# Token-major scores, exponentials turned by DMA, and hand-made orders in an attention and gated feed-forward kernel

## The chip, the cores and the metric

The kernel runs on one core of a Trainium2 chip. The metric is the device time of one execution in microseconds (us); the time of a kernel is the median of its runs. The core's engines work side by side, each through its own list of instructions in order: TensorE (PE in the profile, its weight loads PEld), VectorE (DVE), ScalarE (ACT), GpSimd (POOL) and SyncE (SP), which issues DMA transfers; "SPq" is SP's instruction queue. An instruction waits for the work that it needs, and everything behind it on its engine waits too. PSUM, into which TensorE writes, has eight banks of 128 x 512 numbers.

## The reference

```python
def _attn_ref(q, kv, w_sr):                # q 4 x 12288 x 128, kv 4 x 384 x 32 x 128
    r = 4
    kv_pool = kv.reshape(B, H // r, r, W // r, r, C).mean(axis=(2, 4))
    kv_flat = kv_pool.reshape(B, -1, C) @ w_sr        # 768 keys an image
    k = v = kv_flat
    s = scale * (q @ k.transpose(0, 2, 1))
    a = np.exp(s - s.max(-1, keepdims=True))
    a /= a.sum(-1, keepdims=True) + 1e-09
    return a @ v
def _moe_ref(x, w_gate, w_val, w_out):     # 128 -> 1536 -> 128
    gate = np.maximum(x @ w_gate, 0.0)
    val = x @ w_val
    return gate * val @ w_out
```

Four images of 12,288 query tokens each attend to 768 pooled keys, which are the values too; each token's result goes through a feed-forward layer whose hidden vector is a rectified gate times a value. The layer is of degree two in x: if x is scaled by c, the output is scaled by c squared.

## The kernel before, in words

The 49,152 tokens are cut into 96 tiles of 512, four tiles to a group. All matmul operands are 16 bit. For each tile there are five steps.

- Scores (`scores`, line 290): keys are the weights, the turned queries stream through; the result has keys on the partitions and tokens along the row. Six chunks of 128 keys, one matmul of 512 columns and one exponential on ACT (line 295) each, which writes `aT`.
- Values (`values`, line 297): each 128 x 128 block of `aT` is loaded as weights, and the 128 value columns and a column of ones stream through it, 129 columns. 24 such matmuls a tile; the last column gives the row sums. `keep_sums` and `keep_values` (lines 311 to 324) invert the sums and scale the result on DVE, and `x_turn` (line 326) has SP turn it by a DMA transpose into `xT`.
- Gate and value projections (lines 372 to 390): 12 matmuls of 512 columns each. ACT casts each value block to 16 bit, and DVE forms max(gate, 0) times value into `hT`.
- Output projection (`out_proj`, line 398): 12 matmuls of 512 columns, added up in one bank.
- `out_turn` (line 411): DVE turns the output in 32 x 32 blocks, POOL scales it, and SP stores it in four DMAs.

The first four tiles (`LEAD`) are handled differently: `lead_values` streams `aT` through the values as weights, which gives the result already turned and not divided by the sums; `lead_sums` and `lead_scales` form the squared inverse sums, and `out_turn` multiplies the outputs by them (line 421).

The queries come by POOL's DMAs, cast on the way (`q_load`), and are turned by SP's DMA transposes, one of 128 x 2048 per group (`q_turn`, line 119). The keys of the first image are pooled, turned by TensorE, projected and turned again in an opening whose order is a list of words (`OPENING`, line 69). Those of the other three are made beside the main loop, in pairs of 128-key chunks: four loads of 512 KB (`kv_load`), sums on POOL (`pool_pixels`), 32 x 32 turns on DVE with a detour through DRAM (`turn_blocks`: a write "placed", four reads), a projection by TensorE (`project`), and two lone 128 x 128 DMA transposes for the values (`turn_values_dma`, line 282).

The main loop (line 610) runs once per tile k in twelve steps. In each step the output projection of tile k-4, the value projection of k-3, a score of k or two value chunks of k-1, and the gate projection of k-3 stand in turn, so that TensorE always finds work whose inputs are ready. PSUM banks are handed out in rotation from one pool of eight:

```python
    psum = ctx.enter_context(tc.tile_pool(name="psum", bufs=8, space=bass.MemoryType.PSUM))
    def bank(shape, dtype=FP32):
        return psum.tile(shape, dtype, tag="bank", name="bank_ps")
```

Before the opening's first matmuls, `fill(4)` (line 527) gives TensorE filler work while data comes in.

Of the kernel before, what the change touches and what calls it, by code (L numbers as in the profile page):

```python
# [16 lines left out]
def kernel(  # L17
# [41 lines left out]
    LEAD = GRP  # L59
    qk_scale = 1.0 / math.sqrt(C)  # L60
# [5 lines left out]
        a0:p b0:p p0:p kvT1:a key1:a val1:a a2:p kvT2:a kvT3:a kvT4:a key4:a cast0:p qT1:a  # L66
        cast2:a cast4:p cast5:p xT3:a
    """.split())
    OPENING = """
        T1.0 T1.1 cast1 a0 T1.3 b0 T1.2 kvT1 p0 cast2 pj1 T0.3 cast3 key1 cast0 T0.p kvT0 qt2 a2  # L70
        gate22 W0 W1 cast4 qT4 wo cast5 qT5 qt1 vt1 qt3 qT2 pj0 T3.0 qT1 val1 S1.1 key0 qt0 S2.0
        S2.1 T3.1 V1.1 qT3 qT0 S1.0 S0.1 vt0 b2 val0 S3.1 S0.0 T3.2 V2.1 V0.1 T3.3 kvT3 S3.0
        V1.0 pj3 c2 p2 T2.p kvT2 key3 V0.0 S1.3 vt3 pj2 S3.3 key2 val3 S2.3 V2.0 V1.3 a4 S0.3 a5
        S1.2 S3.2 S2.2 T4.2 p4 b5 T4.p vt2 V0.3 V2.3 T4.3 val2 kvT4 S0.2 c5 p5 V2.2 pj4 V1.2
        T5.p key4 kvT5 S1.4 vt4 S0.4 val4 pj5 S2.4 V0.2 V1.4 key5 S0.5 V0.4 vt5 val5 S3.4 S2.5
        V2.4 S1.5 V0.5 S3.5 U0 xT0 V1.5 v0.2 U1 xT1 R v0.4 V2.5 xT2 v0.5 v0.3 g0.2 v0.0 V3.3
        g0.4 V3.4 v0.1 V3.5 v0.6 g0.3 g0.5 v0.7 v0.10 g0.0 v0.11 g0.10 V3.2 S4.5 S4.2 g0.1 V3.0
        v0.8 S4.0 g0.6 g0.11 v0.9 g0.8 V3.1 xT3 g0.7 S4.4 g0.9
    """.split()
    SUMS = [{"a": [0, 1], "b": ["s", 2]}, {}, {"a": [0, 1], "b": ["s", 2], "c": ["s", 3]}, {}, {"a": [0, 1]}, {"a": [0, 1], "b": ["s", 2], "c": ["s", 3]}]  # L80
# [4 lines left out]
    psum = ctx.enter_context(tc.tile_pool(name="psum", bufs=8, space=bass.MemoryType.PSUM))  # L85

    def bank(shape, dtype=FP32):
        return psum.tile(shape, dtype, tag="bank", name="bank_ps")
# [38 lines left out]
    def q_load_pair(i):  # L127
        q32 = work.tile([128, 2, NS, C], FP32, tag="q32", bufs=2, name="q32")
        nc.sync.dma_start(  # L129
            q32, q[0, i * T : (i + 2) * T, :].rearrange("(p i s) c -> p i s c", i=2, s=NS)  # L130
        )
        for n in range(2):
            q32s[i + n] = q32[:, n]

    def q_load_tile(i):
        q32 = work.tile([128, T], FP32, tag="o_t", bufs=2, name="q32_late")
        nc.sync.dma_start(
            q32, q[0, i * T : (i + 1) * T, :].rearrange("(t j s) c -> j t (s c)", j=4, s=NS)
        )
        q32s[i] = q32.rearrange("p (s c) -> p s c", s=NS)  # L140
# [17 lines left out]
    def q_turned(i):  # L158
        copy_on(f"qT{i}", qTs[0][:, i * NS : (i + 1) * NS, :], q_banks.pop(i))
# [16 lines left out]
    def kv_load(b, pair, lines=range(r), queues=(nc.sync,)):  # L176
        if (b, pair) not in kv_in:
            kv_in[b, pair] = work.tile([128, r, 2, r, C], FP32, tag="kv_in", bufs=3, name="kv_in")
# [4 lines left out]
        for dh in lines:  # L183
            queues[dh % len(queues)].dma_start(  # L184
                parts[:, dh].rearrange("p h dw c -> p (h dw c)"), rows[dh]
            )
# [3 lines left out]
    def pool_pixels(eng, b, pair, h):  # L190
        parts = kv_in[b, pair]
        s2 = work.tile([128, 2, r, C], FP32, tag="kv_s2", bufs=1)
        for i in range(2):
            eng.tensor_tensor(s2[:, i], parts[:, 2 * i, h], parts[:, 2 * i + 1, h], op=ALU.add)  # L194
# [9 lines left out]
    def line(chunk, dh):  # L204
        return kv_in[0, chunk // 2][:, dh, chunk % 2]
# [26 lines left out]
    def turned(name, chunk):  # L232
        kvT = work.tile([128, 128], FP32, tag="kvT_chunk", bufs=3, name="kvT_chunk")
        copy_on(name, kvT, kv_Ts[chunk])
# [8 lines left out]
    def keep_keys(name, jc):  # L243
        pr, engine = key_ps.pop(jc), engine_of(name)
# [9 lines left out]
    def keep_chunk_values(name, jc):  # L254
        copy_on(name, kv16[:, 0, jc, C : 2 * C], value_ps.pop(jc))

    def project(b, pair):
        pr = bank([128, 4, 2, 32])
        nc.tensor.matmul(pr, w_sr_f32, kv_Ts.pop((b, pair)), start=True, stop=True)  # L259
        nc.vector.tensor_scalar(  # L260
            kv16[:, b, 2 * pair : 2 * pair + 2, 0:C].rearrange("c h (i p) -> c h i p", p=32),
            pr.rearrange("c i h p -> c h i p"), 1.0 / (r * r), None, op0=ALU.mult,
        )

    def turn_blocks(b, pair):

        blocks = work.tile([128, 4, 2, 32], FP32, tag="kv_blocks", bufs=2)
# [22 lines left out]
    def scores(k, jc):  # L290
        if k not in aTs:
            aTs[k] = work.tile([128, NJC, T], FP16, tag="aT", bufs=5, name="aT")
        s_ps = bank([128, T])
        nc.tensor.matmul(s_ps, kv16[:, k // NST, jc, 0:C], qT_of(k), start=True, stop=True)  # L294
        nc.scalar.activation(aTs[k][:, jc, :], s_ps, AF.Exp, scale=qk_scale)  # L295

    def values(k, jc, half):
        if jc == 0:
            x_banks[k, half] = bank([128, 2, C + 1])
            if half == 0:  # L300
                x16s[k] = work.tile([128, NS, C], FP16, tag="x16", bufs=3, name="x16")
        x_ps = x_banks[k, half]
        for i in range(2):
            s = 2 * half + i
            nc.tensor.matmul(  # L305
                x_ps[:, i, :], aTs[k][:, jc, s * 128 : (s + 1) * 128],
                kv16[:, k // NST, jc, C : 2 * C + 1],
                start=(jc == 0 and i == 0), stop=(jc == NJC - 1), skip_group_check=True,
            )

    def keep_sums(k, half):
        rinvs[k, half] = work.tile([128, 2, 1], FP32, tag="rinv", bufs=4, name="rinv")
        nc.vector.reciprocal(rinvs[k, half], x_banks[k, half][:, :, C : C + 1])  # L313

    def keep_values(k, half, engine=nc.vector):
        x_ps, rinv = x_banks.pop((k, half)), rinvs.pop((k, half))
        if engine is nc.scalar:
            for i in range(2):
                nc.scalar.mul(x16s[k][:, 2 * half + i, :], x_ps[:, i, 0:C], rinv[:, i])
        else:  # L320
            nc.vector.tensor_tensor(  # L321
                x16s[k][:, 2 * half : 2 * half + 2, :], x_ps[:, :, 0:C],
                rinv.to_broadcast([128, 2, C]), op=ALU.mult,
            )

    def x_turn(k):
        x16 = x16s.pop(k)
        xT = work.tile([128, NS, 128], FP16, tag="xT", bufs=5, name="xT")
        nc.sync.dma_start_transpose(xT, x16.rearrange("p s c -> p (s c)"))
        xTs[k] = xT.rearrange("c s p -> c (s p)")  # L330

# [12 lines left out]
    def lead_kept(name, k):  # L344
        xTs[k] = work.tile([128, NS, 128], FP16, tag="xT", bufs=5, name="xT").rearrange("c s p -> c (s p)")
        copy_on(name, xTs[k], x_banks.pop(k))
# [12 lines left out]
    def lead_scales():  # L359
        turned = work.tile([128, NS * 4, 32], FP32, tag="o_sb", bufs=3, name="sums_turned")  # L360
        nc.vector.transpose(turned.rearrange("p x m -> p (x m)"), x_banks.pop("sums"))
# [9 lines left out]

    def value_proj(k, fb):
        va_ps = bank([128, T])
        nc.tensor.matmul(  # L374
            va_ps, wv16[:, fb * 128 : (fb + 1) * 128], xTs[k], start=True, stop=True
        )
        val = work.tile([128, T], FP16, tag="val", bufs=6, name="val")
        nc.scalar.copy(val, va_ps)  # L378
        vals[k, fb] = val

    def gate_proj(k, fb):
        if k not in hTs:
            hTs[k] = work.tile([128, NFB, T], FP16, tag="hT", bufs=3, name="hT")
        g_ps = bank([128, T])
        nc.tensor.matmul(  # L385
            g_ps, wg16[:, fb * 128 : (fb + 1) * 128], xTs[k], start=True, stop=True
        )
        nc.vector.scalar_tensor_tensor(  # L388
            hTs[k][:, fb, :], g_ps, 0.0, vals.pop((k, fb)), op0=ALU.max, op1=ALU.mult
# [21 lines left out]
    def out_turn(k):  # L411
# [3 lines left out]
        nc.vector.transpose(o_t, o_banks.pop(k))  # L415
# [3 lines left out]
        if k < LEAD:  # L419
            scale = lead_scale[:, k].rearrange("t (s j o) -> t s j o", s=NS, o=1)  # L420
            nc.gpsimd.tensor_tensor(to, o_by, scale.to_broadcast([128, NS, 4, 32]), op=ALU.mult)  # L421
        else:
            nc.gpsimd.tensor_scalar(to, o_by, 1.0 / X_SCALE**2, None, op0=ALU.mult)  # L423
# [19 lines left out]
    def out_scale(k, engine, own, o_ps=None):  # L443
        if k not in o_sbs:
            o_sbs[k] = work.tile([128, NS, 128], FP32, tag="o_sb", bufs=3, name="o_sb")
        o_sb, o_ps = o_sbs[k][:, own], o_ps if o_ps is not None else o_banks[k]
        if engine is nc.scalar:
            nc.scalar.mul(o_sb, o_ps, 1.0 / X_SCALE**2)
        else:
            nc.vector.tensor_scalar(o_sb, o_ps, 1.0 / X_SCALE**2, None, op0=ALU.mult)  # L450
# [51 lines left out]
    nc.sync.dma_start(w_sr_f32, w_sr)  # L502
    q_load_pair(2)
    q_load_pair(0)
    kv_load(0, 1)
    kv_load(0, 2)
    q_load_tile(4)
    q_load_tile(5)

# [17 lines left out]
    fill(4)  # L527
# [4 lines left out]
    def open_step(word):  # L532
# [44 lines left out]
        elif head == "v":  # L577
            value_proj(*at)
        elif head == "g":
            gate_proj(*at)  # L580
        elif head == "W":
# [19 lines left out]
    for word in OPENING:  # L601
# [4 lines left out]
    out_moves, moves = [], []  # L606


    last = NT + LAG - 1
    for k in range(LEAD, last + 1):  # L610
# [9 lines left out]
        at = k % NST - (NST - NJC - 6)  # L620
        for step in range(NFB):
            kO, kF = k - LAG - 1, k - LAG
            half, i = divmod(step // 2, NJC // 2)
            if 0 <= kO:
                out_proj(kO, step)
                if step == NFB - 1 and kO < NT - 3:
                    out_moves = out_turn(kO)
                elif step == NFB - 1 and k < last:
                    out_scale(kO, nc.vector, slice(0, NS))
                    out_store(kO, slice(0, NS))  # L630
            if 2 <= step < 10:
                for _ in range(2):
                    if out_moves:
                        nc.sync.dma_start(*out_moves.pop())
            if kF < NT:
                value_proj(kF, step)
            if step % 2 == 0:
# [61 lines left out]
```

## Time and profile before

| What | Value |
|---|---|
| Median of 7 runs | 1031.51 us (1031.36 to 1032.13) |
| The profiled execution | 1032.13 us |
| Its span, first to last instruction | 1030.3 us |
| Granted TensorE clock | 1.000 |
| DMA moved | 93.33 MB, 91 GB/s on average |
| SP's DMA queue | 312,584 packets, 37.9% of 16 engines |

A line of the costliest groups names the source line, the engine, the operation, the tile written and the tiles read with their shape and number, then busy time in us and mean ns of one, then the idle time of the engine just before these instructions, and what ended it. A line in order of time gives start and duration in us and how many instructions are merged in it. For one source line the profile gives the shortest, median and longest duration in ns. A stretch gives busy us of PE, PEld, DVE, ACT and POOL with instruction counts, then the granted clock, the mean busy share of the 16 DMA engines, and GB/s.

### The profile page before, as it was taken

The numbers are of one execution on the slowest core, as the hardware profiler recorded it, in microseconds if no ns is written. First come the engines' busy times: TensorE is split into PE (matmuls) and PEld (weight loads), VectorE is DVE, ScalarE is ACT, GpSimd is POOL, SyncE is SP. The second block draws the span as 40 slices with busy tenths as digits, with TensorE's granted clock in tenths as the row PEclk, the third lists the DMA queues.
The fourth block names the chain that finished last, engine by engine and source line by source line (L and its number), as shares of the span: only waits on it lengthen the run. The fifth ranks groups of instructions, "written<-read, shape, count | busy, mean of one in ns | idle before, by whom it ended". The sixth has DMA issues, their size and how long they took to land.

```text
span 1030.3 us, 19910 instructions
## 1 busy us (share of the span) xinstructions
PE 1023.3 (99%) x6508; PEld 540.3 (52%) x6508; DVE 909.5 (88%) x1666; ACT 909.1 (88%) x1742; POOL 287.3 (28%) x311
## 2 busy tenths in 40 slices
PE   8999999999999999999999999999999999999998
PEld 5455555555555555555555555555555555555555
DVE  3889898988989888998889898989898888989898
ACT  5988888889888898888988888988888898888987
POOL 3402156511221124742112121664121211111110
PEclk9999999999999999999999999999999999999999
DMA  9935396362652657926356167573552433413122
GB/s 321 116 51 84 97 182 148 72 92 39 88 70 49 73 126 156 167 56 89 51 68 88 32 86 147 138 169 59 84 76 44 73 57 62 87 32 65 34 43 51
DMA packets 327807, 93.33 MB, mean 91 GB/s; under 512 B 307480, under 2 KB 320664, under 8 KB 327704
## 3 DMA queue, kind: packets, MB, share of 16 engines
q1 hardware_dynamic: 312584, 77.97, 37.9%
q0 software_dynamic: 14688, 12.98, 11.3%
q10 hardware_dynamic: 432, 1.11, 0.3%
q8 instruction: 51, 0.84, 0.3%
q14 instruction: 52, 0.43, 0.2%
HBM read 53.94 MB, written 26.35 MB: 78 GB/s over the span
## 4 chain that ended last, share of the span: by engine, by line
PE 96%; DMA 4%; SPq 0%; POOL 0%; issue 0%; ACT 0%; ACTq 0%
PE bank_ps L385 24%; PE bank_ps L374 24%; PE bank_ps L407 23%; PE bank_ps L305 12%; PE bank_ps L294 11%; DMA q_late<-in_q_dram 1%; DMA qT<-q 1%; DMA kv_in<-in_kv_dram 1%; PE bank_ps L393 1%; DMA xT<-x 1%; PE bank_ps L259 0%; SPq L184 0%; SPq L129 0%; SPq L502 0%; POOL q L98 0%
## 5 line engine op out<-in xcount | busy, mean ns | idle before, releaser
L388 DVE SCALAR_TENSOR_TENSOR hT<-bank_ps,val 128x512 f16<-128x512 f32 x1152 | 757.3, 686 | 91.0 <-ACT val L378 70.7
L378 ACT CAST val<-bank_ps 128x512 f16<-128x512 f32 x1152 | 677.7, 589 | 103.8 <-PE bank_ps L374 101.3
L374 PE MATMUL bank_ps<-xT,wv 128*128 128x512 f16 x1152 | 436.9, 380 | 0.5 <-DMA xT<-x 0.5
L385 PE MATMUL bank_ps<-xT,wg 128*128 128x512 f16 x1152 | 436.8, 379 | 0.0
L407 PE MATMUL bank_ps<-hT,wo 128*128 128x512 f16 x1116 | 423.5, 379 | 0.0
L295 ACT ACTIVATE aT<-bank_ps 128x512 f16<-128x512 f32 x576 | 345.3, 603 | 1.7 <-PE bank_ps L294 1.7
L423 POOL TENSOR_SCALAR o_sb<-o_t 128x512 f32<-128x512 f32 x89 | 132.4, 1487 | 665.5 <-DVE rinv L313 653.3
L305 PEld LDWEIGHTS <-aT 128*128 128x128 f16 x2208 | 170.5, 98 | 130.4
L294 PE MATMUL bank_ps<-qT,kv 128*128 128x512 f16 x576 | 216.9, 380 | 0.2 <-DMA qT<-q 0.2
L305 PE MATMUL bank_ps<-kv,aT 128*128 128x129 f16 x2208 | 215.5, 220 | 0.0
L374 PEld LDWEIGHTS <-wv 128*128 128x128 f16 x1152 | 112.5, 98 | 134.2 <-DMA xT<-x 1.0
L385 PEld LDWEIGHTS <-wg 128*128 128x128 f16 x1152 | 112.6, 98 | 68.0
L407 PEld LDWEIGHTS <-wo 128*128 128x128 f16 x1116 | 109.0, 98 | 65.9
L294 PEld LDWEIGHTS <-kv 128*128 128x128 f16 x576 | 56.1, 98 | 67.4 <-DMA qT<-q 0.7
L321 DVE TENSOR_TENSOR x<-bank_ps,rinv 128x256 f16<-128x256 f32 x184 | 78.1, 425 | 6.5
L415 DVE STREAM_TRANSPOSE o_t<-bank_ps 128x512 f32<-128x512 f32 x93 | 65.6, 706 | 0.0
L114 POOL DMA_DIRECT2D q<-in_q_dram x84 | 46.0, 554 | 0.4 <-PE bank_ps L374 0.4
L194 POOL TENSOR_TENSOR s<-kv_in 128x512 f32<-128x512 f32 x36 | 44.8, 1265 | 0.1
L313 DVE RECIPROCAL rinv<-bank_ps 128x2 f32<-128x2 f32 x184 | 26.8, 146 | 0.0
L196 POOL TENSOR_TENSOR s<-s 128x512 f32<-128x512 f32 x18 | 22.8, 1265 | 1.4
L198 POOL TENSOR_TENSOR c<-s 128x256 f32<-128x256 f32 x18 | 13.0, 724 | 1.4
L421 POOL TENSOR_TENSOR o_sb<-o_t,lead_scale 128x512 f32<-128x512 f32 x4 | 4.2, 1046 | 32.2 <-DVE rinv L313 16.2
(68 smaller groups left out, 130.9 us busy)
## 6 DMA issues: line engine op xcount, KB each, us to landing
kv_in<-in_kv_dram SPq DMA_DIRECT2D x46, 512.0 KB, 7.0
out_dram<-o_sb SPq DMA_DIRECT2D x353, 64.0 KB, 2.2
q<-in_q_dram POOLq DMA_DIRECT2D x84, 128.0 KB, 4.7
xT<-x SPq DMA_TRANSPOSE x92, 2.5
out_dram<-o_sb SPq DMA_DIRECT2D x80, 16.0 KB, 1.5
placed<-blocks SPq DMA_DIRECT2D x9, 128.0 KB, 2.5
kvT<-placed SPq DMA_DIRECT2D x36, 32.0 KB, 1.9
kv_in<-in_kv_dram ACTq DMA_DIRECT2D x2, 512.0 KB, 7.1
```

The source lines that it names most:

```text
L114: nc.gpsimd.dma_start(q16[32 * j : 32 * (j + 1)].rearrange("t (i s) c -> t i s c", i=GRP), rows[j])
L294: nc.tensor.matmul(s_ps, kv16[:, k // NST, jc, 0:C], qT_of(k), start=True, stop=True)
L295: nc.scalar.activation(aTs[k][:, jc, :], s_ps, AF.Exp, scale=qk_scale)
L305: nc.tensor.matmul(x_ps[:, i, :], aTs[k][:, jc, s * 128 : (s + 1) * 128], kv16[:, k // NST, jc, C : 2 * C + 1], start=(jc == 0 and i == 0) ...
L321: nc.vector.tensor_tensor(x16s[k][:, 2 * half : 2 * half + 2, :], x_ps[:, :, 0:C], rinv.to_broadcast([128, 2, C]), op=ALU.mult,)
L374: nc.tensor.matmul(va_ps, wv16[:, fb * 128 : (fb + 1) * 128], xTs[k], start=True, stop=True)
L378: nc.scalar.copy(val, va_ps)
L385: nc.tensor.matmul(g_ps, wg16[:, fb * 128 : (fb + 1) * 128], xTs[k], start=True, stop=True)
L388: nc.vector.scalar_tensor_tensor(hTs[k][:, fb, :], g_ps, 0.0, vals.pop((k, fb)), op0=ALU.max, op1=ALU.mult)
L407: nc.tensor.matmul(o_banks[k], wo16[:, fb, :], hTs[k][:, fb, :], start=fb == 0, stop=fb == NFB - 1)
L415: nc.vector.transpose(o_t, o_banks.pop(k))
L423: nc.gpsimd.tensor_scalar(to, o_by, 1.0 / X_SCALE**2, None, op0=ALU.mult)
```

## The change

- From tile 4 on the scores are token-major: `score_block` loads 128 turned queries as weights and streams all 768 keys through, as 512 and 256 columns, into a PSUM tile of two banks; `exp_block` makes one exponential of 768 columns on ACT, which also gives the row sum.
- `a_turn` has SP turn each such 128 x 768 block by a DMA transpose, four a tile. The values are weights now and the turned exponentials stream through, six matmuls of 512 columns, and the result is `xT` after a copy on DVE. It isn't divided by the sums. The x transpose falls away.
- The squared inverse sums are formed once per two tiles (`invert`, `spread_scales`: 16 small copies on POOL), and `out_turn` and `out_scale` multiply the outputs by them.
- The twelve uniform steps are replaced by written orders of words: `STEADY`, `FIRST` (two iterations, which have no values yet), `DRAIN` and `LAST`. o, v, g, x, s, P are matmuls of the output, value and gate projections, values, scores and image projection; y, h, e, kA, pk, oT are the cast, product, exponential, copy of xT, copy of the keys and turn of the output that follow them; tb is the turn of an image pair, r the inversion. The values run two tiles behind the scores, not one.
- Banks: six single ones, each taken from the front of a list to which it returns when what reads it has been written down in the order, and the two-bank score tile, of which there is one. The opening still uses eight.
- Two of a tile's four stores go to POOL's queue. The image chain is spread over four tiles a pair instead of two, with two loads a tile.
- The opening has a new order, other engines for some steps, a fifth filler, and the loads in another order.

The core of the diff:

```diff
+    LAST = [f"{head}{n}" for n in range(NFB) for head in "ovygh"] + ["oT"]
+    FIRST = """
+        r v1 o0 v8 v10 o1 v4 s0 y1 y8 y10 v5 g5 g10 v0 o2 o3 y4 e0 y5 h10 y0 g4 g1 v11
+        o4 h5 y11 s1 e1 o5 h4 g11 g0 v6 g8 h1 y6 o6 h11 v9 h8 o7 y9 h0 s2 e2 g6 v2 v7 h6
+        g9 o8 g7 h9 o9 y7 v3 s3 y2 h7 y3 e3 g2 h2 o10 o11 g3 h3 oT
+    """.split()
...
+    STEADY = """
+        v10 s0 o0 y10 e0 v1 y1 o1 o2 o3 v0 g1 s1 o4 v2 tb y0 v9 o5 o6 e1 h1 g0 g9 y2 g10
+        o7 s2 h0 y9 g2 h10 v7 o8 h9 o9 v3 o10 o11 h2 g7 v8 e2 x1 y7 g8 s3 r oT x5 y3 g3
+        y8 v6 x4 h7 x2 x0 v5 x3 v4 h8 e3 h3 y6 P g5 y5 v11 g11 kA pk g4 y4 h5 y11 g6 h6
+        h11 h4
+    """.split()
...
     def bank(shape, dtype=FP32):
-        return psum.tile(shape, dtype, tag="bank", name="bank_ps")
+        n = next(n for n in free_banks if n < usable[0])
+        free_banks.remove(n)
+        ps = pools[n // 6].tile(shape, dtype, tag=f"bank{n}", bufs=1, name="bank_ps")
+        bank_numbers[id(ps)] = n, ps
+        return ps
...
+    def score_block(k, s):
+        b = k // NST
...
+        s_ps = s_banks[s] = wide.tile([128, 1024], FP32, tag="wide", name="wide_ps")
+        qT = qTs[k // GRP][:, k % GRP * NS + s, :]
+        for j0, j1 in ((0, 4), (4, NJC)):
             nc.tensor.matmul(
...
+                s_ps[:, j0 * 128 : j1 * 128], qT, kv16[:, b, j0:j1, 0:C], start=True, stop=True
             )
...
+    def exp_block(k, s):
+        nc.scalar.activation(
+            a16s[k][:, s, :], s_banks.pop(s)[:, 0:J], AF.Exp, scale=qk_scale,
+            accum_out=a_sums[k // 2][:, k % 2, s : s + 1],
+        )
...
+    def invert(k):
+        inverse = work.tile([128, 2, NS], FP32, tag="inverse", bufs=2, name="inverse")
+        nc.vector.reciprocal(inverse, a_sums.pop(k // 2))
+        square = squares[k // 2] = work.tile([128, 2, NS], FP32, tag="square", bufs=3, name="square")
+        nc.gpsimd.tensor_tensor(square, inverse, inverse, op=ALU.mult)
+
+    def spread_scales(k, j):
...
+        for b in range(4):
+            nc.gpsimd.tensor_copy(
+                to[32 * b : 32 * (b + 1), :, :, j], squares[k // 2][32 * j : 32 * (j + 1)]
             )
...
+    def a_turn(k, s0, s1):
+        aT = aTs[k].rearrange("k j t -> k (j t)").rearrange("k (x p) -> k x p", p=128)
+        nc.sync.dma_start_transpose(
+            aT[:, s0 * NJC : s1 * NJC], a16s[k][:, s0:s1, :].rearrange("p s j -> p (s j)")
+        )
+
+    def values(k, jc):
...
+        nc.tensor.matmul(
+            x_banks[k], kv16[:, k // NST, jc, C : 2 * C], aT[:, jc],
+            start=first, stop=x_left[k] == 0,
+        )
+
+    def keep_values(k):
+        xT = work.tile([128, NS, 128], FP16, tag="xT", bufs=4, name="xT")
         xTs[k] = xT.rearrange("c s p -> c (s p)")
+        nc.vector.tensor_copy(xTs[k], freed(x_banks.pop(k)))
...
-        if k < LEAD:
-            scale = lead_scale[:, k].rearrange("t (s j o) -> t s j o", s=NS, o=1)
-            nc.gpsimd.tensor_tensor(to, o_by, scale.to_broadcast([128, NS, 4, 32]), op=ALU.mult)
-        else:
-            nc.gpsimd.tensor_scalar(to, o_by, 1.0 / X_SCALE**2, None, op0=ALU.mult)
+        scale = scale_of(k).rearrange("t (s j o) -> t s j o", s=NS, o=1)
+        nc.gpsimd.tensor_tensor(to, o_by, scale.to_broadcast([128, NS, 4, 32]), op=ALU.mult)
...
-    fill(4)
+    fill(5)
+    freed(idle)
...
+    def image_step(b, at, step):
+        for pair in range(NJC // 2):
+            since = at - 4 * pair
+            if since in (0, 1) and step in (2, 8):
+                kv_load(b, pair, [2 * since + step // 8])
+            elif since in (2, 3) and step == 3:
+                pool_pixels(nc.gpsimd, b, pair, since - 2)
+            elif since == 5 and moves and step > 4:
+                nc.sync.dma_start(*moves.pop())
+            elif since == 8 and step == 1:
+                turn_values_dma(b, pair)
...
+        at = k % NST - 6
+        kO, kF, kV = k - LAG - 1, k - LAG, k - 2
+        words = FIRST if kV < LEAD else STEADY if k < NT else DRAIN if k < last else LAST
+        for word in words:
...
+            if head == "o":
+                out_proj(kO, n)
+                for queue in (nc.gpsimd, nc.sync):
+                    if out_moves and n >= 2:
+                        queue.dma_start(*out_moves.pop())
+                if spread:
+                    spread_scales(*spread.pop(0))
+                if b < B:
+                    image_step(b, at, n)
...
+            elif head in ("s", "e"):
+                if k < NT:
+                    {"s": score_block, "e": exp_block}[head](k, n)
+                    if head == "e":
+                        a_turn(k, n, n + 1)
```

In the opening's list, a word such as T0.1 turns line 1 of chunk 0 of the first image by four matmuls (a sum, T1.p, takes two); before it has 11 of the first kind and four sums, after it 14 and three. S, V, v and g are the scores, values, value and gate projections of the first tiles; four scores of tile 4 that stood in the opening are in the loop now.

## The prediction

> **What bounds the kernel now.** I read the engine totals of the page first, then the matmuls in order of time, then the costliest groups, then the DMA queue of SyncE (SP). The profiled execution took 1032.13 us with a span of 1030.3, so 1.8 us lie around it; the median is 1031.51, 0.6 below.
>
> ```profile
> PE 1023.3 (99%) x6508; PEld 540.3 (52%) x6508; DVE 909.5 (88%) x1666; ACT 909.1 (88%) x1742; POOL 287.3 (28%) x311
> ```
>
> TensorE is never idle for long. Busy time does not say that it runs at its peak, so I looked at when matmuls start:
>
> ```profile
> 500.24 0.38 PE L374 MATMUL bank_ps<-xT,wv 128*128 128x512 f16 x1
> 500.45 0.39 PE L305 MATMUL bank_ps<-kv,aT 128*128 128x129 f16 x4
> 500.68 0.38 PE L385 MATMUL bank_ps<-xT,wg 128*128 128x512 f16 x1
> ...
> 501.97 0.38 PE L374 MATMUL bank_ps<-xT,wv 128*128 128x512 f16 x1
> ```
>
> The 0.38 is a latency; the starts count. Over the trace a 512-column matmul follows the last after 216 ns, a 129-column one after 56.7 ns. A tile has 42 of the first (36 projections, 6 scores) and 24 of the second: 42 x 0.216 + 24 x 0.0567 = 9.07 + 1.36 = 10.43 us, and the tiles start 10.42 to 10.43 us apart (10.86 where an image pair is projected). So the steady part is TensorE work without gaps, and only TensorE work, or a new wait of TensorE, can move it. One gap is there after the opening: 0.7 us at 434 us, for an x transpose that took 8.0 us to land.
>
> ```profile
> L388 DVE SCALAR_TENSOR_TENSOR hT<-bank_ps,val 128x512 f16<-128x512 f32 x1152 | 757.3, 686 | 91.0 <-ACT val L378 70.7
> L378 ACT CAST val<-bank_ps 128x512 f16<-128x512 f32 x1152 | 677.7, 589 | 103.8 <-PE bank_ps L374 101.3
> L295 ACT ACTIVATE aT<-bank_ps 128x512 f16<-128x512 f32 x576 | 345.3, 603 | 1.7 <-PE bank_ps L294 1.7
> ...
> L321 DVE TENSOR_TENSOR x<-bank_ps,rinv 128x256 f16<-128x256 f32 x184 | 78.1, 425 | 6.5
> L415 DVE STREAM_TRANSPOSE o_t<-bank_ps 128x512 f32<-128x512 f32 x93 | 65.6, 706 | 0.0
> ```
>
> ScalarE (ACT) and VectorE (DVE) are at 88% and wait for TensorE. Their means overlap too: starts of cast and exponential are 0.485 us apart when queued, of the gating products 0.60.
>
> ```profile
> L329 SPq DMA_TRANSPOSE xT<-x x92: 1188/1214/2790, 57.7 to 1009.9; - x92
> L124 SPq DMA_TRANSPOSE qT<-q x22: 1914/3963/5876, 44.2 to 928.9; - x22
> L284 SPq DMA_TRANSPOSE kv<-kv x18: 1126/1226/2009, 185.6 to 732.7; - x18
> L634 SPq DMA_DIRECT2D out_dram<-o_sb x432: 315/618/2206, 48.3 to 1019.8; - x144
> ```
>
> These (shortest/median/longest ns) are what an issue holds SP for; 4, 16 and 1 blocks of 128x128 in the transposes.
>
> **TensorE's part.** Removed per tile: six score matmuls and 24 value matmuls, 6 x 0.216 + 1.361 = 2.657 us. Added: six value matmuls of 512 columns, 1.296, and four score blocks of 512 + 256 columns. The 256-column one is not in the trace; between 129 columns (0.0567) and 512 (0.216) a straight line gives 0.110, so 4 x 0.326 = 1.304. The tile becomes 10.37 us, 0.057 less; 92 tiles: **-5.2 us**. The operands become strided (keys four blocks at a time, turned exponentials in four pieces); the query transposes feed 4 x 32 patterns at the full rate in this trace, so I add nothing (0 to +1 us).
>
> [...] The trace has each with its own weight load at 56.7 ns. The row decides: there is no weight-load stall to win back.
>
> **The transposes, and a rule against them.** Each tile's 24 blocks now go through SP, four issues of six blocks; the x transpose (1.21) goes. [...] L284 is such a lone block, 1.13 to 1.23; but four cost 1.21 and sixteen 3.64 undisturbed (at 341.85 us). Six lie between 3.64 x 6/16 = 1.37 and the line through both, 1.62; I take 1.5 since neither row is nearer. SP's tile: 4 x 1.5, a quarter of a query transpose 1.0, two stores instead of four (the others go to POOL) 1.3, waits 0.3: 8.6 of 10.37 us. The transfers themselves: 256-byte packets of an undisturbed x transpose take 19.7 ns in the packet records, 3,072 x 19.7 / 16 engines = 3.8 us a tile, on a DMA share of 0.24 in the last stretch without image work, of which 0.6 us goes.
>
> ```profile
> 900.00:1000.00 100.00, 100.00 (x634) 52.31 (x632) 89.53 (x164) 89.89 (x174) 13.39 (x9) 1.00 0.24 43
> ```
>
> About 0.55 then, and up to 0.9 where before showed 0.6 with image loads. What covers this is distance: the last of four transposes of tile k is issued late in its iteration (e3 stands behind 9.3 of 10.37 us of matmuls), the first value matmul of k comes two iterations on (x1, behind 6.6 us). 2 x 10.37 + 6.6 - 9.3 = 18 us, less 2.5 for landing: some 15.5 us. Cost: 0; without that cover every us late is a us of TensorE. The x transpose of before had less cover, so its 0.7 us gap goes: **-0.7**.
>
> **Image chain.** Over 17 of 24 tiles of three batches, per pair: four loads 2.4 us, one placement 0.4, four reads 1.8, two lone transposes 2.4; the reads now follow the placement within one matmul or two, so SP stands for its landing, about 2.5, with the second exponential transpose behind it. Three pairs: 28.5. SP: 17 x 8.6 + 28.5 = 175 us, against 17 x 10.37 = 176. It stays level, and runs behind by several us around each placement, inside the 15.5. The pooling sums (5 us per chunk) keep their engine, POOL: with two stores (0.7 each), the output scaling (1.05 in the row of the lead tiles, in place of 1.49) and on even tiles 16 small copies at 0.19, up to 10.6 us in two of four tiles and half that in the others. A late scaling holds the store behind it on SP, so it also draws on the 15.5. Cost 0, to +15 (rival 2).
>
> **ScalarE.** Twelve casts stay, 12 x 0.485 = 5.82. Six exponentials become four of 768 columns: 0.485 plus 256 columns at the slope of its 512- and 128-column rows (604 and 277 ns: 0.85 ns each) is 0.70; 2.8. Sum 8.6 (8.7 before), plus four times the row sum, which no row shows. Below: 0, if the sum comes along. Above: the one-column ACTIVATE of 0.203 plus the lost overlap 603 - 485, 0.32. I take 0.2, as the one-column row is the nearest: 9.4 of 10.37. It reaches TensorE only above (10.37 - 8.6)/4 = 0.44. The single two-bank score tile makes each score block wait for the exponential before it; in the list seven or more matmuls, 1.5 us, lie between, against 0.9 and 0.17 for the hand-over. The image projection takes the same tile once a pair; its copy stands behind kA, and the next score block starts some 0.5 us after it. Cost 0, except in the two FIRST iterations, which have no value matmuls: 9.1 us of TensorE against 9.4 of ScalarE: **+0.6**.
>
> **VectorE.** Two reciprocals and two scalings (2 x (0.18 + 0.34) by their starts) become one cast, 0.61, and half a reciprocal: 8.9 to 8.5 us a tile. It was not on the path: 0.
>
> **Banks.** Six single banks instead of eight. Counting along STEADY, six are held at x1, g8 and v4. Each next matmul takes the bank freed longest ago: after g8 that of oT (product queue done about 0.6 us before it is needed), after v4 that of h8 (about 1.1). The tightest is g6 on the cast kA, about 0.3. Cost 0; at 0.05 a tile the gain is gone.
>
> **Opening and end.** Before, TensorE starts the image at 7.32 us and reaches the loop at 37.66, with 26.1 us of work and some 4 us of gaps, six of 0.4 to 0.5. A fifth filler adds two short halves, 0.86; 14 x 4 + 6 turning matmuls instead of 44 + 8 add 10 x 0.109 = 1.1. The new order turns two chunks at once while data lands. If it halves the gaps it is level; all or none of them give -2 to +2. I take **0**. The four output scalings of tile 94 on ScalarE (4 x 0.28 instead of 0.60) lie under the last 48 matmuls; the last stores are as before: 0.
>
> Sum: -5.2 - 0.7 + 0.6 = -5.3; 1032.1 - 5.3 = 1026.8 against the profiled execution, **1026.2** against the median.
>
> **Rivals.**
> 1. *Small waits eat the gain* (14%). The bank hand-offs of 0.3 us turn into waits of 0.04 to 0.07 us a tile, or the opening keeps its gaps: 1029.5 to 1033.5, say 1031. For: only 0.057 us a tile is won. Against: before runs hundreds of tiles without a gap, and the list leaves each hand-off some slack.
> 2. *SP falls behind in the image stretches* (12%), the case on the other side. My 175 us holds undisturbed issues; L124 shows 3.64 to 5.88, L329 up to 2.79. From 176 + 15.5 = 192 us, 9% above mine, TensorE waits. At 197 it is 5 us a batch, 15 in all: 1041. For: SP is level with no reserve there. Against: loads are now two a tile instead of four at once.
> 3. *ScalarE becomes the bound* (8%): if a row sum costs two one-column instructions and the overlap, 0.52, a tile takes 10.7 and the total is 1026 + 92 x 0.32 = 1055. Against: nothing shows more than one.
> That the steps aren't what they say is ruled out by the counts; only the opening may do nothing.
>
> **How the numbers follow.** The forecast holds at 1024 to 1028.5 with 62%; 4% below it (opening gaps closed). A measurement tells 0.2%, 2.1 us, from no change: 1029.4 to 1033.6. Faster 62 + 4 = 66%, same 14, slower 12 + 8 = 20. Range 1023 to 1040: it leaves out rival 3 and the upper half of rival 2.
>
> **What would show it.** Right: tiles 10.37 us apart, no wait of TensorE for a bank, for aT or for the score tile; ScalarE near 90%; SP's gaps closed only in image stretches. Wrong: value matmuls waiting for a transpose (rival 2, only in image tiles), score blocks for the exponential in every tile (rival 3), tiles of 10.40 to 10.45 with waits for banks (rival 1); the loop reached later than its work says (opening).

## The result

The changed kernel takes 1035.98 us in the median of 15 runs (1031.81 to 1040.27), the one before in the same session 1031.75: a ratio of 1.0039, 95% interval 1.003 to 1.0048. It is 0.4% slower, where 0.5% faster was forecast, and its runs scatter over 8 us where those of before stay within 1.4. The profiled execution took 1034.9 with a span of 1033.1.

Engine totals of the changed kernel:

```profile
PE 1022.4 (99%) x5048; PEld 489.1 (47%) x5048; DVE 863.0 (84%) x1432; ACT 920.2 (89%) x1931; POOL 524.4 (51%) x1308
```

TensorE is as busy as before and the rest has room, so the totals don't show the loss. Two stretches do (busy us of PE, PEld, DVE, ACT, POOL with counts, granted clock, DMA share, GB/s):

```profile
100.00:200.00 100.00, 95.85 (x454) 44.76 (x453) 81.05 (x136) 85.34 (x180) 63.38 (x132) 0.98 0.95 169
400.00:500.00 100.00, 98.26 (x475) 46.56 (x474) 84.93 (x143) 89.14 (x188) 52.85 (x133) 1.00 0.89 147
```

In the other stretches of 100 us behind the opening TensorE is busy for 99.9 to 100. What it waited for in the loop is one line (us in all, times, longest):

```profile
PE bank_ps L399 <- DMA aT<-a: 5.8, 3, 3.7
```

Its matmuls in order of time, in the first of the two stretches:

```profile
177.03 0.38 PE L453 MATMUL bank_ps<-xT,wv 128*128 128x512 f16 x1
181.11 0.41 PE L399 MATMUL bank_ps<-aT,kv 128*128 128x512 f16 x1 [3.70 <-DMA aT<-a]
181.33 0.63 PE L466 MATMUL bank_ps<-xT,wg 128*128 128x512 f16 x1
181.74 0.85 PE L357 MATMUL wide_ps<-kv,qT 128*128 128x512 f16 x2
182.38 0.63 PE L399 MATMUL bank_ps<-aT,kv 128*128 128x512 f16 x1
182.81 0.64 PE L466 MATMUL bank_ps<-xT,wg 128*128 128x512 f16 x1
```

The first value matmul of a tile stands 3.7 us for its turned exponentials. After the pause matmuls of 512 columns follow each other in 0.427 us instead of 0.216, until 184.5, so the stop costs more than its own length. Tile by tile, the tiles are 10.36 to 10.37 us apart (10.80 with an image projection, the one matmul of the loop whose operands are 32 bit), but one takes 16.34 and one 12.69; over the loop some 8 us lie in such places. Without them this execution would have taken about 1027.

What SP does ahead of the wait:

```profile
164.51 0.59 SPq L736 DMA_DIRECT2D out_dram<-o_sb  x1
165.14 0.64 SPq L223 DMA_DIRECT2D kv_in<-in_kv_dram  x1
166.16 0.59 SPq L736 DMA_DIRECT2D out_dram<-o_sb  x1
166.86 0.55 SPq L321 DMA_DIRECT2D placed<-blocks  x1
170.60 0.78 SPq L712 DMA_DIRECT2D kvT<-placed  x2
171.47 2.08 SPq L389 DMA_TRANSPOSE aT<-a  x1
173.61 1.04 SPq L712 DMA_DIRECT2D kvT<-placed  x2
174.69 0.62 SPq L223 DMA_DIRECT2D kv_in<-in_kv_dram  x1
175.42 1.24 SPq L389 DMA_TRANSPOSE aT<-a  x1
```

A placement is issued, SP stands 3.2 us until it has landed, and three transposes of tile 15 queue behind; SP is done with the last at 178.1, it lands at 181.0 and is used at 181.1. I took from the trace how long before the first value matmul of each tile SP was done with its last transpose; call this the margin. Undisturbed it is 17.6 us. In the image stretches it sinks to about 3 at tiles 11, 15, 41 and 43, and to 5.6 in the third stretch. From there to the landing took 1.8 to 4.6 us at the tiles with the least margin, and TensorE waited at tiles 14 (0.4), 15 (3.7) and 43 (1.7).

The issues of SP, shortest, median and longest in ns, and the exponential of ScalarE with the row sum, which is an instruction of its own:

```profile
L389 SPq DMA_TRANSPOSE aT<-a x368: 1209/1244/3606, 40.2 to 998.8; - x184
...
L154 SPq DMA_TRANSPOSE qT<-q x22: 1848/4970/6398, 47.9 to 927.5; - x22
...
L362 ACT ACTIVATE a<-wide_ps x368: 810/811/857, 39.2 to 997.8; 128x768 f16<-128x768 f32 x184
L362 ACT ACTIVATION_READ_ACCUMULATOR a<-wide_ps x368: 194/195/236, 39.9 to 998.5; 128x1 f32 x184
```

### The profile page after: what moved, and what is told of

It is laid out like the page before. It is cut to its first block, busy times and chain, and to the rows that moved or that the text cites. A ratio compares the mean times of both kernels' runs of the same rounds, so it can differ in the third digit from the quotient of the medians.

```text
span 1033.1 us, 18011 instructions
## 1 busy us (share of the span) xinstructions
PE 1022.4 (99%) x5048; PEld 489.1 (47%) x5048; DVE 863.0 (84%) x1432; ACT 920.2 (89%) x1931; POOL 524.4 (51%) x1308
## 2 busy tenths in 40 slices
DMA packets 480500, 153.55 MB, mean 149 GB/s; under 512 B 456720, under 2 KB 470544, under 8 KB 480400
## 4 chain that ended last, share of the span: by engine, by line
PE 96%; DMA 2%; ACT 1%; DVE 0%; issue 0%; POOL 0%; SPq 0%; POOLq 0%; DVEq 0%
PE bank_ps L453 24%; PE bank_ps L466 23%; PE bank_ps L494 23%; PE bank_ps L399 12%; PE wide_ps L357 11%; DMA aT<-a 2%; PE bank_ps L613 1%; PE bank_ps L266 1%; PE bank_ps L480 1%; PE bank_ps L342 1%; PE bank_ps L416 1%; PE wide_ps L298 0%; DVE hT L474 0%; ACT a L362 0%; DMA kvT<-placed 0%
## 5 line engine op out<-in xcount | busy, mean ns | idle before, releaser
L494 PE MATMUL bank_ps<-hT,wo 128*128 128x512 f16 x1116 | 348.7, 379 | 0.0
L362 ACT ACTIVATE a<-wide_ps 128x768 f16<-128x768 f32 x368 | 302.0, 821 | 51.2 <-PE wide_ps L357 51.2
L399 PE MATMUL bank_ps<-aT,kv 128*128 128x512 f16 x552 | 179.8, 381 | 6.0 <-DMA aT<-a 5.8
L357 PE MATMUL wide_ps<-kv,qT 128*128 128x512 f16 x736 | 180.2, 327 | 0.1
L507 POOL TENSOR_TENSOR o_sb<-o_t,scale 128x512 f32<-128x512 f32 x89 | 93.4, 1049 | 133.6 <-issue 119.2
L383 POOL COPY scale<-square 32x8 f32<-32x8 f32 x736 | 141.4, 192 | 28.6
L736 POOL DMA_DIRECT2D out_dram<-o_sb x216 | 134.7, 627 | 19.0 <-POOL o_sb L507 13.0
L357 PEld LDWEIGHTS <-qT 128*128 128x128 f16 x736 | 72.0, 98 | 87.4 <-issue 0.7
L407 DVE CAST xT<-bank_ps 128x512 f16<-128x512 f32 x92 | 63.6, 692 | 33.9 <-PE bank_ps L399 33.9
L362 ACT ACTIVATION_READ_ACCUMULATOR a<-wide_ps 128x1 f32 x368 | 75.9, 206 | 0.0
```

Of the source, the lines that this page charges most:

```text
L357: nc.tensor.matmul(s_ps[:, j0 * 128 : j1 * 128], qT, kv16[:, b, j0:j1, 0:C], start=True, stop=True)
L362: nc.scalar.activation(a16s[k][:, s, :], s_banks.pop(s)[:, 0:J], AF.Exp, scale=qk_scale, accum_out=a_sums[k // 2][:, k % 2, s : s + 1],)
L383: nc.gpsimd.tensor_copy(to[32 * b : 32 * (b + 1), :, :, j], squares[k // 2][32 * j : 32 * (j + 1)])
L399: nc.tensor.matmul(x_banks[k], kv16[:, k // NST, jc, C : 2 * C], aT[:, jc], start=first, stop=x_left[k] == 0,)
L494: nc.tensor.matmul(o_banks[k], wo16[:, fb, :], hTs[k][:, fb, :], start=fb == 0, stop=fb == NFB - 1)
L736: queue.dma_start(*out_moves.pop())
```

## The experiments

The theory: in the image stretches SP's queue has more to issue and to stand for than the time of its tiles, so the transposes come late. Rivals: the 16 DMA engines are full there, so that fewer issues would not help; POOL, which pools, scales and stores, holds SP up; or the loss lies elsewhere (banks, opening) and the waits are a side show.

**Without image work.** The image step, the turn, the projection and its copy are left out, and all tiles use the first image's keys.

```diff
-                if b < B:
-                    image_step(b, at, n)
...
-                if b < B and 0 <= pair < NJC // 2 and since == 0:
+                if False:
```

> Leaves out the image chain of the main loop (loads, pooling, turns, projection of images 2 to 4; all tiles attend to the first image's keys). First theory, SP's queue falls behind in the image stretches: no wait for a turned exponential is left, tiles 10.37 us apart throughout, and without nine projections of 0.43 us the time is 1026 - 4 = 1022 us. The rival that the opening or the bank hand-offs eat the gain: the nine projections go and nothing else, 1036 - 4 = 1032.

Measured: 1023.34 (1023.16 to 1023.75), ratio 0.9919 (0.9902 to 0.9935). No wait of TensorE for a transpose is left, and the tiles are 10.365 us apart from end to end:

```profile
100.00:200.00 100.00, 100.00 (x484) 47.15 (x482) 85.00 (x141) 91.52 (x194) 42.84 (x123) 1.00 0.79 129
```

With the nine projections of 0.43 us that were left out, this makes 1027.2. So the excess comes with the image work, not from banks or the order of the words. The run takes the bytes away with the issues (DMA share 0.79 instead of 0.95), so it can't tell these two apart.

**Reads one iteration later.**

```diff
-            elif since == 5 and moves and step > 4:
+            elif since == 6 and moves and step > 4:
```

> Moves the four reads that follow the placement one iteration later, so that SP no longer stands for the placement's landing (23.7 us over nine pairs in the trace of the change). First theory, SP is late: some 9 us less standing in each image stretch, the margin of the transposes stays above 3 us, the waits go, 1026 to 1029. Rival, the 16 DMA engines are full in those stretches (share 0.95 to 1.01): no byte is moved less, still about 1036.

Measured: 1028.94 (1025.99 to 1032.69), ratio 0.9976 (0.9967 to 0.9985). The margin of the transposes stays at 4.2 us or more and no value matmul waits. But a new wait is in the profile, now for the late reads themselves:

```profile
PE wide_ps L298 <- DMA kvT<-placed: 3.8, 1, 3.8
```

SP's delay has moved from one reader to the other. That speaks for the theory, though not cleanly. The profiled execution is one of the slow end, 1032.33, and its granted clock is 0.998; of the 18 runs the six with 0.998 took 1030.79 to 1032.69 and the twelve with 1.000 took 1025.99 to 1029.98. In this trace a granted clock below 1.000 is the mark of such a pause (last section); that it is so in the other runs is likely, but they left no trace.

**Stores from POOL, stores from SP.** All four stores of a tile from one queue (in the first the first and last group stay as they were):

```diff
-                for queue in (nc.gpsimd, nc.sync):
+                for queue in (nc.gpsimd, nc.sync if kO <= GRP or kO >= NT - 4 else nc.gpsimd):
```

```diff
-                for queue in (nc.gpsimd, nc.sync):
+                for queue in (nc.sync, nc.sync):
```

> All four stores of a tile from POOL's queue instead of two (first and last group as before). SP issues two stores less a tile, 1.26 us; POOL two more. First theory, SP is late: in the image stretches SP needs 47 - 5 = 42 us for four tiles of 41.5, the margin holds, 1025 to 1029. Rival, the DMA engines are full: the same bytes, 1036. Third theory, POOL holds SP up: POOL has more to do, so slower than 1036.

> All four stores from SP's queue, none from POOL's. First theory, SP is late: 2.5 us more a pair of stores, 5 us for four tiles; in image stretches 52 us against 41.5, some 30 us behind per batch with 15 us of margin, so 15 or more us a batch of waiting: 1070 or more. Rival, the DMA engines are full: the same bytes, 1036. Third theory, POOL holds SP up: a little faster than 1036.

Measured: 1026.84 (1026.65 to 1027.3), ratio 0.9953 (0.9938 to 0.9968), and 1088.97 (1087.58 to 1093.42), ratio 1.0562 (1.0539 to 1.0585). Two issues a tile more or less on SP decide it. That POOL holds SP up is out: it has more to do in the faster one. With all stores on SP, TensorE's waits are those of the theory:

```profile
PE bank_ps L399 <- DMA aT<-a: 43.9, 15, 5.0
```

With the stores on POOL the critical stretches are closed, though the DMA engines are no less busy:

```profile
100.00:200.00 100.00, 99.75 (x482) 47.25 (x480) 86.26 (x144) 90.48 (x191) 76.84 (x159) 1.00 0.99 178
400.00:500.00 100.00, 100.00 (x484) 47.55 (x483) 85.44 (x144) 91.24 (x193) 62.41 (x143) 1.00 0.88 148
```

**Half the bytes of the image loads.** Only the first half of each row is read, `rows[dh][:, :, 0 : r * C]`, and pooled twice.

> The changed kernel, but the image loads of the main loop carry half the bytes with the same number of issues (both chunks of a pair are pooled from the first half, so the second half of images 2 to 4 is left out). SP's issues stay, 9.4 MB of 153.6 go, all of it in the image stretches. Theory, SP is late: its issues last nearly as long, the waits stay, 1033 to 1036. Rival, the DMA engines are full: a good part of the waits goes, 1027 to 1030.

Measured: 1027.49 (1026.99 to 1029.09), ratio 0.9962 (0.9948 to 0.9975): the number of the rival. It speaks for full DMA engines; the theory had 1033 to 1036. The trace says why both are partly right. From the last transpose of tile 34 to that of 43 SP takes 99.5 us instead of 109.3; an exponential transpose holds it for 1.35 us in the mean instead of 1.46, a store 0.62 instead of 0.69, a query transpose 4.8 instead of 5.9, and the landing of placements 6.0 instead of 8.1. The DMA share of the stretch from 400 to 500 us is 0.86 instead of 0.89 (that of the first 0.84 instead of 0.95): in this pair of runs more load on the DMA engines goes with longer issues and landings.

**Query loads apart from query transposes.**

```diff
         if ph == 1:
             q_turn(g + 1)
+        if ph == 3:
             q_load(g + 2)
```

> The changed kernel, with the query loads of POOL two tiles away from the query transpose of SP instead of beside it. Same bytes, same issues. The query transpose holds SP for 4.97 us in the median, 3.64 when alone. Theory, SP is late and contention stretches its issues: 1.3 us less for four tiles, some 4 us in a stretch, fewer waits, 1030 to 1033. If the stretching is no part of it: 1036.

Measured: 1035.56 (1033.74 to 1036.34), ratio 1.0035 (1.0021 to 1.0048). Not the 1030 to 1033 expected. The query transpose does fall:

```profile
L154 SPq DMA_TRANSPOSE qT<-q x22: 1316/2385/3437, 48.1 to 926.3; - x22
```

But in the same nine tiles the exponential transposes rise to 1.49 in the mean, placements from 0.8 to 1.2, and the standing for their landing from 8.1 to 9.4: 106.0 us instead of 109.3. In the first stretch nothing is gained (the least margin is 2.7). It looks as if the load stretched other issues instead; that this is the reason isn't shown.

**Two blocks to an issue.** This one takes issues away and leaves every byte of the data (153.49 MB moved instead of 153.55, with 1.2% fewer packets).

```diff
-                        a_turn(k, n, n + 1)
+                        if n % 2:
+                            a_turn(k, n - 1, n + 1)
```

> The changed kernel, with the exponentials of two score blocks turned by one issue of twelve blocks, two issues a tile instead of four. The same bytes in the same packets, fewer issues. An issue of six blocks holds SP for 1.21 us at the shortest, one of four too, and one of sixteen 2.4 in the median where no query load runs beside it, so twelve should take about 1.9: 3.8 instead of 5.4 us a tile, 6 us less in four tiles. Theory, SP's queue is late: the waits go, 1026 to 1028. Rival, the DMA engines are full: no byte less, 1036.

Measured: 1026.63 (1026.16 to 1026.82), ratio 0.9952 (0.9939 to 0.9966). At the shortest and in the median twelve blocks hold SP hardly longer than six (1.21 and 1.24 us in the changed kernel):

```profile
L389 SPq DMA_TRANSPOSE aT<-a x184: 1273/1463/6287, 42.6 to 990.7; - x184
```

```profile
100.00:200.00 100.00, 100.00 (x484) 47.53 (x483) 85.99 (x145) 90.98 (x193) 67.35 (x149) 1.00 0.98 175
400.00:500.00 100.00, 100.00 (x485) 47.59 (x483) 85.49 (x142) 91.19 (x193) 49.50 (x122) 1.00 0.83 150
```

In the nine loaded tiles of above twelve take 2.28 in the mean, against 1.46 for six, which still makes 41 us of transposes instead of 53; SP takes 93.5 us instead of 109.3, as long as TensorE needs, and over the whole loop the margin stays at 8.5 or more. The DMA share of the first stretch is 0.98, more than the 0.95 with the waits, and TensorE has none. So it is SP's queue that is late, and busy DMA engines only as far as they stretch it.

**Both.** Two blocks to an issue and the stores on POOL.

> Two blocks per issue, and the stores from POOL as in the run that had no waits (1026.8). If TensorE's work is all that is left, 1026.8 again; if waits for late transposes still cost something there that the profile doesn't show, less.

Measured: 1026.81 (1026.19 to 1027.42), ratio 0.9956 (0.9943 to 0.9968). Nothing more is to be had there: TensorE's work is left. Two blocks to an issue alone, two changed lines, beats both kernels.

**The opening.** On the version with the stores on POOL, once the opening of before (order, engines, loads, `fill(4)`), once only `fill(4)`:

> All stores but those of the first and last group from POOL (1026.8, no waits in the loop), with the opening of before: its order without the four scores of tile 4, its engines, its loads, four fillers. The prediction has the new opening level: 1026 to 1027.6. Rival, the new opening gains by closing gaps: 1028 or more. Other rival, it loses, as its work grew by 2 us: 1025.5 or less.

> All stores but those of the first and last group from POOL (1026.8), with four fillers instead of five. If TensorE's work sets the opening, two halves of 0.43 us less: 1026.0. If the landing of the image lines sets it: 1026.8.

Measured: 1028.19 (1027.88 to 1028.43) and 1026.82 (1026.21 to 1028.35), against 1026.84. In this loop the new order, engines and loads gain about 1.3 us over the old; the fifth filler costs nothing.

## Why the prediction was wrong

- **TensorE's part held.** Tiles 10.365 us apart were forecast at 10.37; 512 columns follow after 216 ns, 256 after 109 (forecast 110). The strided operands cost nothing. The 0.7 us gap of before is gone.
- **ScalarE held**, at 8.6 us and four sums of 0.2: the sum is an instruction of 0.195 behind an exponential of 0.81, ScalarE is busy 91% of the steady stretches, and no wait of TensorE for it shows. Rival 3 fell; so did rival 1, since no bank is waited for.
- **The two FIRST iterations** took 9.27 and 9.71 us; with the shifted place of the first output matmul (0.3) that is about 0.5 over 2 x 9.06, forecast 0.6.
- **The opening** was put at 0 and gained 1.3 against the old one in the same loop. Against the kernel before it is less clear: the first output matmul starts at 37.7 us there, at 37.0 in the changed kernel and at 36.5 to 37.4 in the runs without waits.
- **The image chain is the step that failed**: "SP: 17 x 8.6 + 28.5 = 175 us, against 17 x 10.37 = 176. It stays level". The parts were near, the average was not. The loads, placements, reads and lone transposes of three pairs do not spread over 17 tiles; most fall into ten. From the last transpose of tile 33 to that of 43 SP had eight loads, three placements, twelve reads and four lone transposes. By the prediction's own prices that is 86 + 23.7 = 110 us against 104 of TensorE; it took 118.5, 102.0 of issues and 16.5 in which SP issued nothing. So about 6 us of the lack stood in the prediction's own prices, hidden by the mean over 17 tiles, and 9 more were mis-sized. The largest of these is the time between issues: 8.3 us besides the placements' landing, most of it in 84 gaps of 0.08, where "waits 0.3" a tile makes 3.0. Then the two query transposes, 11.8 instead of 10, the placements' issues, 2.4 instead of 1.2, the stores, 13.9 instead of 13, and the landing, 8.1 instead of 7.5. The 1.5 for six blocks is near the 1.46 of these tiles by luck: the median over the loop is 1.24, and the line behind the 1.5 was wrong (last section).
- **The margin was taken as full everywhere.** Undisturbed it is as worked out (17.6 us to the issue's end, forecast 18). But at tile 6, where the first stretch begins, it is 9.7: in iterations 5 to 8 the first group's outputs go out in 16 stores a tile, eight from SP, which the prediction charges to no one. With all sixteen on SP (the run with SP's stores) it is 2.7 there. From 9.7 the margin is at 3.1 by tile 11, behind the first pair's placement; in the second stretch, from 16.2 at tile 34, it takes until tile 41.
- **Rival 2 is what happened**, at 1036, and was given 12%. Its 1041 came from 5 us of waiting in each of three batches; in the trace the first lost about 6.5 us, the second 1.9 and the third nothing. Its sum counted waits alone, but a stop of 3.7 us cost about 1.7 more, as 3.4 us of matmuls at half rate followed.

Without SP's delay the rest of the sum stands: 1026.63 and 1026.84 measured, 1026.2 forecast.

## What to carry to other kernels

Add up the queue that issues transfers by stretch, not by the mean of a phase, with what it stands for and how far behind it already is when the stretch begins. Two tiles of distance hid the transposes of this kernel only while the queue ahead of them kept up: with the margin at 17.6 us TensorE did not wait, at 3.0 (tile 15) it waited 3.7. Here fewer issues for the same bytes relieved the queue more (93.5 us for the nine tiles) than half the bytes of the image loads with the same issues did (99.5).

## What was not expected of the hardware

- At the shortest a DMA transpose held SP for 1.13 us with one block of 128 x 128 (before, L284), 1.19 with four (before, L329), 1.21 with six, 1.27 with twelve (two blocks to an issue) and 1.32 with sixteen (query loads apart): from one block to sixteen it rises by 0.19 us of 1.32, so nearly all of it is here the price of the issue, not of its blocks. Under load it grows, to 2.28 in the mean with twelve and to 5.9 with sixteen. The straight line through four and sixteen blocks that the prediction drew was wrong, because its 3.64 of sixteen, at 341.85, was no undisturbed issue: POOL had begun the query loads at 341.39. Apart from them the median is 2.39 instead of 4.97.
- Pauses of TensorE were followed by matmuls at half rate, and not by their length alone. In the first two lines, of the changed kernel, the granted clock goes from 1.00 to 0.50 behind the pause at 181, and the matmuls of 512 columns from 216 to 427 ns; in the other two, of the version with all stores on SP, it does so behind a pause of 2.50 us:

```profile
177.91:181.32 3.41, 0.21 (x1) 0.13 (x2) 0.47 (x1) 0.12 (x1) 2.13 (x2) 1.00 1.24 235
181.32:184.73 3.41, 3.41 (x10) 1.36 (x9) 1.38 (x2) 1.49 (x3) 3.25 (x7) 0.50 0.74 141
510.68:514.09 3.41, 0.91 (x5) 0.32 (x4) 1.34 (x3) 0.92 (x2) 1.05 (x1) 1.00 0.82 159
514.09:517.50 3.41, 3.41 (x10) 1.18 (x8) 1.38 (x2) 1.49 (x3) 0.00 (x0) 0.50 0.54 96
```

In that version a pause of 3.14 us (at 468) was followed by the full rate. In the loops of the four traces with pauses (these two, the reads later and the query loads apart) the halved stretches last 3.41 us and, within a trace, begin whole multiples of 3.41 us apart. On that grid all twelve pauses that left 2.21 us or more of the 3.41 of one stretch idle were followed by one halved stretch; none of the eight others over 0.9 us, which left at most 1.79 of a stretch idle, was. By my estimate a halved stretch costs about 1.7 us, half of its 3.41. The granted clock of the execution is 0.998, that of the version with all stores on SP, with nine such stretches, 0.986. Of the 15 runs of the changed kernel 14 show 0.996 to 0.998, and the fastest, 1031.81, shows 1.000.
